# Attention with a gelu MLP on one core: the first group's maxima moved ahead of its exponentials, four groups' repeated parts written by copies inside DRAM

## Chip, cores and metric

The kernel runs on one core of one Trainium2 chip. The metric is the device time of one execution in microseconds (us); the time before is a median of three runs. An engine executes its instructions in the order in which they were written; the engines wait for each other by semaphores. TensorE is PE in the profile, its weight load PEld, VectorE DVE, ScalarE ACT, GpSimd POOL, and SyncE, which issues all DMAs here, SP.

## The reference, cut to what matters

`x` has 2048 rows of 512. `a` is attention with 32 heads of width 16, where each query sees itself and the 255 keys before it; `b` is a gelu MLP with 1792 hidden columns.

```
qkv = x @ wqkv                         # 2048 x 1536
p   = softmax(where(0 <= i - j < 256, q k^T / 4, -1e9))
a   = (p v) @ wo
b   = gelu(x @ w1 + b1) @ w2 + b2
g   = sigmoid((x * gate_w).sum(-1))
out = g * a + (1 - g) * b
```

## The kernel before, in words

All products are in a split form: a value is kept as a high part and the rest, and `mm3` (lines 108 to 110) multiplies high by high, high by rest and rest by high into the same sums. Lines 108 to 110 are therefore most of the PE work: q and k (tiles `qk`), v (`v`), the first MLP layer (`u`), the second (`y`) and the output projection (`a`).

**Stages.** The rows are four tiles of 512 (`t` = 0 to 3). `qkv(t)` transposes x (`xp`, line 261), makes q, k and v and stores them in DRAM. `qk_out` turns one 128-column piece `j` of q or k into two parts on ACT and DVE (tile `qke`, lines 322 and 325) and stores three: both parts (line 329), and the high part once more (line 330), so that the three products of the split form can later be stacked along the contraction axis. In SQ and SK the index `i` (0 to 3) is the piece: groups of four heads 0 to 3 read `i` 0 and 1, groups 4 to 7 read `i` 2 and 3. The space of `ks`, `qd` and `qs` serves as x transposed for `t` = 0, 1 and 2, and is cleared and loaded for attention afterwards.

**Attention** goes through eight groups of four heads, each in 16 blocks (`kb`) of 128 keys or queries, four instructions (`i`) per block. First the row maxima: `att_max` multiplies `qd` and `kd` (tile `sm`, line 519) and DVE takes the maximum under the mask (tile `jm`, line 524, with a small read-out row). `att_rows` negates and transposes four blocks' maxima (lines 536 to 539), and eight small casts on POOL put them as rows into `qs` (line 546). Then `att_exp` multiplies `qs` and `ks`, so that the maximum is taken off inside the product (tile `st`, line 564), ACT takes the exponential (tile `pt`, line 586), POOL cuts the band's corners (line 580), and `att_pvs` multiplies by v (line 608). `st`, `sm` and `d` (which holds `qk`, `u` and `y`) have 3, 3 and 2 buffers in PSUM.

**Order.** It is written out by hand with a counted clock. `fill(ns)` takes the next pieces of the dense work (qkv, then the MLP as `mlp`, then `final`) for that many ns; `after(ns, fn)` puts a step into a list that is worked off when the counted clock reaches it. The dense work runs alone for `START` = 105000 ns; `qd` is loaded `AHEAD` = 9000 ns before its end. The loop runs over `u` from -`LEAD` = -12: at each step it issues the maxima of block `u` + 12 and, from `u` = 0, the exponentials of block `u`; a quarter of `STEP0` (`u` below 0) or `STEP` is filled with dense work after each. In the MLP's first layer (`stage` "u") instructions go one by one, otherwise in pairs. So maxima stay 12 blocks ahead of exponentials all along, also at the start.

**The MLP's gelu** for one `u` tile has four ACT steps (x1 line 719, square 722, tanh 728, high part 734) and three DVE steps (725, 731, 737); x1 has two buffers. **Weights**: a raw weight tile is loaded (line 170), copied on ACT (178), and its rest taken on DVE or POOL (182, `split`). POOL takes odd tiles as long as the counted clock at the load is below `RAWS` = 152000; after it all go to DVE, with two raw buffers.

**DMAs** are all issued by SP in one order, with eight semaphores in turn: a DMA waits until the one eight before it has landed. `load_kd`, `load_qd`, `load_ks`, `load_qs` and `att_load_v` are written at fixed places of the loop; the first `load_ks` pair stands in `qkv(2)`, behind its pieces 8 and 9.

Of the kernel before, what the change touches and what calls it, by code (L numbers as in the profile page):

```python
# [19 lines left out]
NT = S // T  # L20
NB = T // 128
# [11 lines left out]
def gated_mix(ctx: ExitStack, tc: tile.TileContext, x, wqkv, wo, w1, b1, w2, b2, gate_w, out):  # L33
    nc = tc.nc
# [11 lines left out]
    def f32(ap):  # L46
        return ap.bitcast(F32)
# [187 lines left out]
    def clear_q(i):  # L235

        v = qd[:, i // 2, i % 2]
        nc.scalar.activation(v, nil.broadcast_to([128, 2 * T]), AF.Copy)

    xts, xrs = {}, {}  # L240

    def load_xr(t, bs=range(NB)):
# [71 lines left out]
    def qk_out(t, j, p):  # L314

        dst, i = (SQ[t], j) if j < NC else (SK[t], j - NC)
        e = sb.tile([128, 2, T], F32R, tag="h", bufs=7, name=f"qke{t}_{j}")

        h = 1 if j < NC else 0

        def hi():
            nc.scalar.activation(e[:, h], p, AF.Copy)  # L322

        def lo():
            nc.vector.tensor_sub(e[:, 1 - h], p, f32(e[:, h]))  # L325

        def store():
            to = dst[:, :, :, i].rearrange("h d s c -> (h d) s c")
            nc.sync.dma_start(to[:, 0:2], f32(e))
            nc.sync.dma_start(to[:, 2], f32(e[:, h]))  # L330
            done.add(("qk", t, j))
        after(100, hi), after(700, lo), after(700 + HOLDQ, store)

# [36 lines left out]
    def qkv(t):  # L370
# [30 lines left out]
        for n, (kind, j) in enumerate(pieces):  # L401
            if not last and XAT <= n < XAT + NC:
                nc.sync.dma_start(XT[t][n - XAT], f32(xts[t][:, n - XAT]))
            if kind == "qk":
                need(("w", (kind, j)))
            else:
                need(*[("w", ("v", c)) for c in range(NC)])
            if t == 0 and n == 10:
                nc.sync.dma_start(b1c, b1.rearrange("(f p) -> p f", p=128))
            if t == 0 and n < 2:  # L410
                pass
            elif kind == "qk":
                yield from qkv_qk(t, j)
            else:
                yield from qkv_v(t, j)
            if t == 1 and n % 3 == 2:
                clear_k(n // 3)
            if t == 2 and n < 4:
                clear_q(n)
            if t == 2 and n in (1, 2):  # L420
                load_kd(0, n - 1)
            if t == 2 and n in (8, 9):
                load_ks(0, n - 8)
            if t == 0:
                for i in ([2], [3], [4], [5], [6], [7, 8], [9, 10], [11])[n] if n < 8 else []:
                    split(keys[i], nc.vector if i % 2 else nc.gpsimd)
                if n == 1:
# [12 lines left out]
            if not last and n == xat[-1] + 1:  # L440
                gate(t + 1)
# [481 lines left out]
    for c in (0, 1):  # L923
        load_qd(0, c)
    fill(AHEAD)
    for u in range(-LEAD, NU):
        m = u + LEAD
        gm, bm = divmod(m, NKB)
        step = STEP if u >= 0 else STEP0
        for i in range(4):  # L930
            if i == 1 and m % NB == 0 and NB <= m < NU - NB:
                load_kd(*divmod(m // NB + 1, NT)), load_qd(*divmod(m // NB + 1, NT))
# [6 lines left out]
            for op, i in [(op, k) for k in pair for op in ORDER[:3]] + [("f", k) for k in pair]:  # L939
                if op == "s" and u >= 0:  # L940
                    att_exp(u // NKB, u % NKB, i)
                if op == "m" and m < NU:
                    att_max(gm, bm, i ^ XOR)
                if op == "p" and i == PVAT and u >= 1:
                    att_pvs(u - 1)
                if op == "f":
                    fill(step / 4)
        if m < NU and bm % RB == RB - 1:
            after(900, att_rows, gm, bm // RB)
        if m % NB == QAT % NB and QAT <= m < QAT + NKB:  # L950
            load_qs(0, (m - QAT) // NB)
# [18 lines left out]
WARM = (9, 4)  # L970
RB = 4
NKB = S // 128
PTS = 7
RAWS = 152000.0
PUT = 1200
LEAD = 12
QAT = 5
START = 105000.0
NORM = 6000
YSWAP = 3  # L980
GELU = (700, 1500, 3600, 4600, 6000, 7000)
XAT = 3
ORDER = 'mspf'
XOR = 1
PACE = 4000.0
LAND = 7500.0
# [6 lines left out]
DIVS = ((8000, 10000, 16000, 23000, 25000), (4500, 5700, 8500, 17000, 18500))  # L993
REST = 1000.0
MXAT = 5500.0
AHEAD = 9e3
STEP0 = 2750.0
PVAT = 2
STEP = 2330.0
# [20 lines left out]
```

## Time and profile before

| | us |
|---|---|
| median of three runs (lowest, highest) | 750.44 (749.94, 751.40) |
| the profiled execution's own time | 750.61 |
| its span | 748.9 |
| PE busy | 734.0 (98%) |
| DVE busy | 520.6 (70%) |
| ACT busy | 421.7 (56%) |
| POOL busy | 372.4 (50%) |
| DMA: moved, share of 16 engines | 170.97 MB, 81.3% |

The span runs from the first to the last instruction; 1.7 us of the execution lie around it. In a timeline a row has the start, the duration, the engine, the line, the operation, output<-input with shapes, a count, and in brackets how long the engine was idle before it and what ended that. Matmul rows overlap (a 512-column one is shown with 0.39 us, the next starts 0.23 us later), so prices of PE are taken from start to start.

### The profile page before, as it was taken

The page shows a single profiled execution, that of the slowest core. Times are in us where ns is not written, and L with a number is a line of the kernel's source. Part 1 is how long each engine was busy: PE and PEld are TensorE (multiplying, and loading weights), DVE is VectorE, ACT ScalarE, POOL GpSimd, SP SyncE. Part 2 cuts the span into 40 slices and gives each one's busy share as a digit, 9 for nine tenths or more (in the row PEclk, how much of TensorE's full clock was granted, in tenths as well). Part 3 has the DMA queues.
Part 4 walks back from the last instruction along what each step waited for, and adds up shares of the span by engine and source line. Part 5 has one row for each costly group of instructions (what it writes and reads, how often), then busy time and mean ns, then how long its engine had stood idle before and what let it go on. Part 6 is the DMA issues. An engine that isn't in the chain of part 4 may idle for free.

```text
span 748.9 us, 17963 instructions
## 1 busy us (share of the span) xinstructions
PE 734.0 (98%) x6129; PEld 606.7 (81%) x6129; DVE 520.6 (70%) x1567; ACT 421.7 (56%) x972; POOL 372.4 (50%) x846
## 2 busy tenths in 40 slices
PE   9999999998999999999999999999999999999998
PEld 7888888876788888888887887888888888878787
DVE  4532325799768867986798689768867886784552
ACT  4434532358537845764695478447735853784541
POOL 4200000339756865876587567747765875630000
PEclk9999999999999999999999999999999999999999
DMA  9889798997995777799676989996799799438682
GB/s 316 329 268 407 257 392 277 273 312 182 273 251 133 172 229 211 176 227 249 164 174 152 241 215 230 259 235 155 171 268 244 180 238 239 136 88 262 217 287 106
DMA packets 179259, 172.12 MB, mean 230 GB/s; under 512 B 56672, under 2 KB 122976, under 8 KB 179168
## 3 DMA queue, kind: packets, MB, share of 16 engines
q1 hardware_dynamic: 179168, 170.97, 81.3%
q8 instruction: 49, 0.80, 0.5%
q14 instruction: 42, 0.34, 0.2%
HBM read 108.53 MB, written 62.39 MB: 228 GB/s over the span
## 4 chain that ended last, share of the span: by engine, by line
PE 84%; DMA 4%; DVE 4%; ACT 3%; issue 3%; SPq 1%; POOL 1%; DVEq 0%; ACTq 0%; POOLq 0%
PE sm L519 9%; PE st L564 8%; PE pv_sm L608 7%; PE y L108 6%; PE y L109 6%; PE y L110 6%; PE u L108 6%; PE u L109 5%; PE u L110 5%; PE qk L110 4%; PE qk L108 4%; PE qk L109 4%; PE pv_st L608 2%; PE a L108 2%; PE v L108 2%
## 5 line engine op out<-in xcount | busy, mean ns | idle before, releaser
L524 DVE CUSTOM_DVE_ANT_0 jm<-sm,mask 128x320 bf16<-128x320 f32 (+4 forms) x512 | 238.0, 465 | 95.6 <-PE sm L519 61.2
L580 POOL TENSOR_SCALAR_AFFINE_SELECT pt<-pt 64x256 f32<-64x256 f32 (+1 forms) x538 | 228.1, 444 | 108.6 <-ACT pt L586 98.1
L586 ACT ACTIVATE pt<-st 128x320 f32<-128x320 f32 (+4 forms) x512 | 199.6, 424 | 138.7 <-PE st L564 136.1
L519 PE MATMUL sm<-kd,qd 96*128 96x320 f32 (+4 forms) x512 | 154.1, 312 | 6.0 <-DVE M L524 5.1
L564 PE MATMUL st<-qs,ks 128*128 128x320 f32 (+4 forms) x512 | 154.4, 309 | 1.7 <-ACT pt L586 1.7
L546 POOL CAST qs<-tt 4x256 fp32r<-4x256 f32 x256 | 124.2, 485 | 52.7 <-DVE tt L539 42.0
L519 PEld LDWEIGHTS sm<-kd,qd 96*128 96x128 f32 x512 | 96.5, 188 | 32.8 <-DVE M L524 13.5
L564 PEld LDWEIGHTS st<-qs,ks 128*128 128x128 f32 x512 | 97.5, 190 | 18.5 <-ACT pt L586 2.9
L108 PE MATMUL y<-w,h 128*128 128x512 f32 x224 | 88.6, 395 | 0.0
L109 PE MATMUL y<-w,h 128*128 128x512 f32 x224 | 88.1, 393 | 0.0
L110 PE MATMUL y<-w,h 128*128 128x512 f32 x224 | 87.9, 393 | 0.0
L108 PE MATMUL u<-mx,w 128*128 128x512 f32 x196 | 80.0, 408 | 0.0
L109 PE MATMUL u<-mx,w 128*128 128x512 f32 x196 | 77.4, 395 | 0.0
L110 PE MATMUL u<-mx,w 128*128 128x512 f32 x196 | 77.1, 393 | 0.0
L608 PE MATMUL pv_st<-pt,vbuf 64*32 64x320 f32 (+4 forms) x1408 | 73.3, 346 | 1.5 <-ACT pt L586 1.0
L608 PE MATMUL pv_sm<-pt,vbuf 64*32 64x320 f32 (+4 forms) x1408 | 74.2, 347 | 0.2
L608 PEld LDWEIGHTS pv_sm<-pt,vbuf 64*32 64x32 f32 x1408 | 51.2, 106 | 19.3 <-issue 2.2
L325 DVE TENSOR_TENSOR qke<-qk,qke 128x512 fp32r<-128x512 f32 x32 | 22.0, 689 | 46.9 <-ACT qke L322 31.1
L322 ACT ACTIVATE qke<-qk 128x512 fp32r<-128x512 f32 x32 | 19.1, 598 | 56.2 <-PE qk L110 30.3
L110 PEld LDWEIGHTS y<-w,h 128*128 128x128 f32 x224 | 42.1, 188 | 9.8
L608 PEld LDWEIGHTS pv_st<-pt,vbuf 64*32 64x32 f32 x1408 | 46.2, 106 | 1.8 <-ACT pt L586 1.1
L338 POOL MEMSET vx<- 128x32 f32 x16 | 2.4, 155 | 88.9 <-DMA SK<-qke 30.7
(148 smaller groups left out, 1334.7 us busy)
## 6 DMA issues: line engine op xcount, KB each, us to landing
kd<-SK SPq DMA_DIRECT2D x32, 384.0 KB
qs<-SQ SPq DMA_DIRECT2D x64, 192.0 KB
mx<-XT SPq DMA_DIRECT2D x24, 512.0 KB
SQ<-qke SPq DMA_DIRECT2D x16, 512.0 KB
SK<-qke SPq DMA_DIRECT2D x16, 512.0 KB
ND<-nd SPq DMA_DIRECT2D x32, 256.0 KB
raw_w<-in_B_w_dram SPq DMA_DIRECT2D x28, 256.0 KB
ks<-SK SPq DMA_DIRECT2D x32, 192.0 KB
```

The lines of the kernel that those rows point to most:

```text
L108: nc.tensor.matmul(p, lh, rh, start=first, stop=False)
L109: nc.tensor.matmul(p, lh, rl, start=False, stop=False)
L110: nc.tensor.matmul(p, ll, rh, start=False, stop=last)
L322: nc.scalar.activation(e[:, h], p, AF.Copy)
L325: nc.vector.tensor_sub(e[:, 1 - h], p, f32(e[:, h]))
L519: nc.tensor.matmul(p[:, :w], qd[0:96, n, pr, 128 * j:128 * (j + 1)], kd[0:96, n, pr, k1 - w:k1], start=True, stop=True)
L524: nc.vector.tensor_tensor_reduce(junk[:, :w], p[:, :w], mask[:, 320 - w:320], 1.0, -3e38, ALU.add, ALU.max, M[:, 2 * (b % RB) + hb, pr:pr ...
L546: nc.gpsimd.tensor_copy(dst, src.unsqueeze(1).broadcast_to([4, 2, RB, 32]))
L564: nc.tensor.matmul(p[:, :w], ks[:, slot(g_, kb // NB), pr, at:at + 128], qs[:, pr, k0:k0 + w], start=True, stop=True)
L580: nc.gpsimd.affine_select(out=v, in_=v, pattern=[[0, v.shape[1]], [1 - 2 * e, 64]], compare_op=ALU.is_ge, fill=0.0, base=-e, channel_multi ...
L586: nc.scalar.activation(pt[:, hf, pr, :w], p[:, :w], AF.Exp, scale=SCALE)
L608: nc.tensor.matmul(pv[r // 64][32 * i:32 * i + 32, q - c * T:e - c * T], vts[g_, b // NB][r:r + 64, v:v + 32], rhs(r), start=start, stop=s ...
```

## The change

Three things change, and the numbers that set their places:

- **Maxima.** The loop now starts at `u` = -16. A counter `made` and `next_max` issue maxima one by one. Before `u` = 0 all 64 maxima of the first group are issued (`4 * NKB`); from `u` = 0 a maximum is issued only when fewer than `4 * (u + 12)` + its place have been made. So none stands in blocks `u` = 0 to 3, and from `u` = 4 the maxima are 12 blocks ahead again. `START` goes from 105000 to 94000, `AHEAD` to 10000. `att_rows` comes 1400 ns after a quarter's last maximum instead of 900 ns after the whole step; the first group's `load_qs` come after blocks 5, 9, 13 and 15 instead of 5, 9, 13 and 17.
- **k's first stacks.** The first two `load_ks` move from `qkv(2)` to `qkv(3)`, behind its pieces 5 and 6 (the v tiles 1 and 2).
- **Copies.** For `i` = 2 and 3 (what groups 4 to 7 read) the repeated high part is no longer stored from SBUF. Sixteen DMAs copy it inside DRAM, from the part already stored, at counted times 188000, 196000 and so on to 308000.

```
-            nc.sync.dma_start(to[:, 2], f32(e[:, h]))
+            if i < 2:
+                nc.sync.dma_start(to[:, 2], f32(e[:, h]))
+                done.add(("qk", t, j))
+            else:
+                copies[0] += 1
+                after(COPY0 + COPY * copies[0] - now[0], copy, to)
+
+        def copy(to):
+            nc.sync.dma_start(to[:, 2], to[:, h])
             done.add(("qk", t, j))
...
-            if t == 2 and n in (8, 9):
-                load_ks(0, n - 8)
+            if last and n in (5, 6):
+                load_ks(0, n - 5)
...
-    for u in range(-LEAD, NU):
-        m = u + LEAD
+    made = [0]
+    def next_max():
+        m, i = divmod(made[0], 4)
+        made[0] += 1
         gm, bm = divmod(m, NKB)
+        if i == 1 and m % NB == 0 and NB <= m < NU - NB:
+            load_kd(*divmod(m // NB + 1, NT)), load_qd(*divmod(m // NB + 1, NT))
+        att_max(gm, bm, i ^ XOR)
+        if i == 3 and bm % RB == RB - 1:
+            after(1400, att_rows, gm, bm // RB)
+        if i == 3 and m in QAT:
+            after(600, load_qs, 0, QAT.index(m))
+    for u in range(-NKB, NU):
...
+            for k in pair:
+                if made[0] < (4 * (u + LEAD) + k + 1 if u >= 0 else 4 * NKB) and made[0] < 4 * NU:
+                    next_max()
+                if u >= 0:
+                    att_exp(u // NKB, u % NKB, k)
+                if k == PVAT and 1 <= u:
+                    att_pvs(u - 1)
+            for k in pair:
+                fill(step / 4)
...
+COPY0 = 180000.0
+COPY = 8000.0
-QAT = 5
-START = 105000.0
+QAT = (5, 9, 13, 15)
+START = 94000.0
-AHEAD = 9e3
+AHEAD = 10e3
```

**PE, at the first exponentials.** Before, from the first `st` on, each `st` (block, place) has an `sm` beside it; the `u` rows are the MLP's first layer:

```order
L519 MATMUL sm_12_1_1770<-kd,qd 128x320
L564 MATMUL st_0_0_1774<-qs,ks 128x320
L108 MATMUL u_2_1740<-xt_1009,w_2_1418 128x512
L109 MATMUL u_2_1740<-xt_1009,w_2_1418 128x512
L110 MATMUL u_2_1740<-xt_1009,w_2_1418 128x512
L519 MATMUL sm_12_0_1789<-kd,qd 128x320
L564 MATMUL st_0_1_1794<-qs,ks 128x320
L519 MATMUL sm_12_3_1797<-kd,qd 128x320
L564 MATMUL st_0_2_1802<-qs,ks 128x320
```

The same place in the changed kernel:

```order
L528 MATMUL sm_15_2_1827<-kd,qd 128x320
L108 MATMUL u_2_1806<-xt_1001,w_2_1476 128x512
L109 MATMUL u_2_1806<-xt_1001,w_2_1476 128x512
L110 MATMUL u_2_1806<-xt_1001,w_2_1476 128x512
L573 MATMUL st_0_0_1838<-qs,ks 128x320
L108 MATMUL u_2_1806<-xt_1001,w_2_1476 128x512
L109 MATMUL u_2_1806<-xt_1001,w_2_1476 128x512
L110 MATMUL u_2_1806<-xt_1001,w_2_1476 128x512
L573 MATMUL st_0_1_1848<-qs,ks 128x320
L573 MATMUL st_0_2_1850<-qs,ks 128x320
```

The 16 `sm` of blocks 12 to 15 have moved ahead of `st_0_0`; up to the `sm` just ahead of `st_4_0`, the next group's first, there is none. From `st_4_0` on PE's order is the same in both kernels.

**POOL, at the same place** (casts of row maxima into `qs`, a weight's rest, band corners of `pt`). Before:

```order
L182 TENSOR_TENSOR w_1_1749<-raw_w_1633,w_1_1749 128x512
L546 CAST qs<-tt 4x2x4x32 x2
L580 AFFINE_SELECT pt_0_1773<-pt_0_1773 64x4x64 x4
L546 CAST qs<-tt 4x2x4x32 x6
L182 TENSOR_TENSOR w_3_1884<-raw_w_1734,w_3_1884 128x512
L580 AFFINE_SELECT pt_1_1842<-pt_1_1842 64x4x64 x4
```

In the changed kernel:

```order
L182 TENSOR_TENSOR w_1_1815<-raw_w_1702,w_1_1815 128x512
L555 CAST qs<-tt 4x2x4x32 x2
L589 AFFINE_SELECT pt_0_1837<-pt_0_1837 64x4x64 x4
L555 CAST qs<-tt 4x2x4x32 x5
L589 AFFINE_SELECT pt_1_1883<-pt_1_1883 64x4x64 x4
L555 CAST qs<-tt 4x2x4x32
```

The rest of weight tile `w_3` is off POOL: its load now comes after the counted 152000, and DVE takes it. The casts here are those of the first group's last quarter; before, they were the third quarter's, and the last quarter's stood behind the corners of `pt_3`.

**SP, at the first load for the maxima** (XT is a store of x transposed, SQ and SK stores of q and k, `qd` and `ks` loads, SV stores of v). Before:

```order
L403 DMA XT_93<-qs 128x1024
L329 DMA SK_85<-qke_6_1035 128x2x512
L330 DMA SK_85<-qke_6_1035 128x512
L329 DMA SQ_81<-qke_3_1054 128x2x512
L330 DMA SQ_81<-qke_3_1054 128x512
L329 DMA SK_85<-qke_7_1079 128x2x512
L330 DMA SK_85<-qke_7_1079 128x512
L480 DMA ks<-SK_83 48x8x128
L475 DMA ks<-SK_83 48x7x128
L477 DMA ks<-SK_83 48x2x64
L357 DMA SV_89<-vx_0_1080 128x272
```

In the changed kernel:

```order
L412 DMA XT_93<-qs 128x1024
L489 DMA qd<-SQ_79 48x8x128
L484 DMA qd<-SQ_79 48x7x128
L486 DMA qd<-SQ_79 48x2x64
L489 DMA qd<-SQ_80 48x8x128
L484 DMA qd<-SQ_80 48x7x128
L486 DMA qd<-SQ_80 48x2x64
L330 DMA SK_85<-qke_6_1026 128x2x512
L330 DMA SQ_81<-qke_3_1050 128x2x512
L330 DMA SK_85<-qke_7_1074 128x2x512
L366 DMA SV_89<-vx_0_1075 128x272
```

The `qd` loads, which came 18 DMAs behind that store of XT, now follow it directly; the repeated parts and `ks` are gone from this place.

More of the change, by code (lines that the diff above doesn't have):

```diff
@@ L238, in clear_q @@
         nc.scalar.activation(v, nil.broadcast_to([128, 2 * T]), AF.Copy)
+    copies = [0]
     xts, xrs = {}, {}
@@ L925, in gated_mix @@
     fill(AHEAD)
-    for u in range(-LEAD, NU):
-        m = u + LEAD
+    made = [0]
+    def next_max():
+        m, i = divmod(made[0], 4)
+        made[0] += 1
         gm, bm = divmod(m, NKB)
+        if i == 1 and m % NB == 0 and NB <= m < NU - NB:
[6 more added lines that the diff above has]
+    for u in range(-NKB, NU):
         step = STEP if u >= 0 else STEP0
         for i in range(4):
-            if i == 1 and m % NB == 0 and NB <= m < NU - NB:
-                load_kd(*divmod(m // NB + 1, NT)), load_qd(*divmod(m // NB + 1, NT))
             if i % 2 == 0:
@@ L938, in gated_mix @@
                 pair = (i,)
[L939 to L944, printed above, removed]
-                    att_pvs(u - 1)
[L946 to L951, printed above, removed]
+            for k in pair:
[4 more added lines that the diff above has]
+                if k == PVAT and 1 <= u:
+                    att_pvs(u - 1)
+            for k in pair:
+                fill(step / 4)
         if u % NB == 0 and NB <= u < NU - NB:
@@ L982 @@
 XAT = 3
-ORDER = 'mspf'
 XOR = 1
```

## The prediction

> **What bounds the kernel now.** I read the page first: the span, the shares of the engines and the slices over time.
>
> ```profile
> span 748.9 us, 17963 instructions
> PE 734.0 (98%) x6129; PEld 606.7 (81%) x6129; DVE 520.6 (70%) x1567; ACT 421.7 (56%) x972; POOL 372.4 (50%) x846
> ...
> PE   9999999998999999999999999999999999999998
> ...
> DVE  4532325799768867986798689768867886784552
> ACT  4434532358537845764695478447735853784541
> ```
>
> PE sets the time. It is idle for 748.9 - 734.0 = 14.9 us of the whole span, so an edit that adds no PE work and takes none away can win that much at most, and only where the idle time lies in a place that it touches. One slice is 18.7 us. The first one that is not 9 is the tenth (168 to 187 us), and there DVE stands at 9 and ACT at 8. The profiled execution took 750.61 us, 1.7 more than its span and 0.17 more than the median of 750.44. I work from 750.61 and take the 0.17 off at the end.
>
> Next I asked for the busy time in four stretches: the maxima before the first exponential, the first `st` of block 0 to the last of block 4, the rest of that stage, and the time in which the copies will run. The columns are the length, then busy us of PE, PEld, DVE, ACT and POOL with counts, the granted clock, the DMA share and GB/s.
>
> ```profile
> 160.75:184.50 23.75, 20.91 (x161) 15.49 (x159) 22.18 (x63) 19.27 (x42) 18.25 (x32) 1.00 0.83 198
> 184.50:200.00 15.50, 14.53 (x112) 12.37 (x118) 13.15 (x43) 9.78 (x23) 11.97 (x27) 1.00 0.89 282
> 124.00:160.00 36.00, 36.00 (x173) 30.44 (x172) 28.12 (x102) 13.40 (x35) 10.93 (x21) 1.00 0.99 308
> 200.00:345.00 145.00, 144.93 (x1426) 121.60 (x1405) 111.57 (x370) 87.49 (x204) 99.23 (x232) 1.00 0.81 202
> ```
>
> From 124 to 160 us PE has no gap at all, although the DMA share is 0.99: the full DMA queues of the qkv stage cost PE nothing. From 160.75 to 184.50 PE is idle for 2.84 us and DVE is 93% busy; ACT has 4.48 us free (23.75 - 19.27). Here the change can win. The timeline of PE says who ends the waits:
>
> ```profile
> 160.60 0.31 PE L519 MATMUL sm<-kd,qd 96*128 96x320 f32 x1
> 160.75 0.32 PE L564 MATMUL st<-qs,ks 128*128 128x320 f32 x1
> 160.90 0.40 PE L108 MATMUL u<-xt,w 128*128 128x512 f32 x1
> ...
> 161.61 0.31 PE L519 MATMUL sm<-kd,qd 96*128 96x320 f32 x1
> ...
> 162.71 0.42 PE L519 MATMUL sm<-kd,qd 96*128 96x320 f32 x1 [0.65 <-DVE M L524]
> ...
> 167.42 0.41 PE L564 MATMUL st<-qs,ks 128*128 128x320 f32 x1 [0.30 <-ACT pt L586]
> ...
> 171.80 0.38 PE L564 MATMUL st<-qs,ks 128*128 128x320 f32 x1 [0.40 <-ACT pt L586]
> ...
> 176.53 0.42 PE L519 MATMUL sm<-kd,qd 96*128 96x320 f32 x1 [0.64 <-DVE M L524]
> ...
> 178.81 0.30 PE L519 MATMUL sm<-kd,qd 96*128 96x64 f32 x1 [0.44 <-DVE M L524]
> ...
> 181.73 0.24 PE L608 MATMUL pv_st<-nil,vbuf 64*32 64x64 f32 x1
> ```
>
> Four of the waits are `sm` for a PSUM buffer that DVE has not read yet or `st` for one that ACT has not read: both engines are near their limit, DVE more so.
>
> **The change, part by part.**
>
> **1. Maxima moved ahead of `st_0_0`.** By the order of PE, 15 `sm` of 320 columns that stood behind the first `st` now stand ahead of it (64 against 49). One costs 160.75 - 160.60 = 0.15 us, so `st_0_0` comes 15 x 0.15 = 2.25 us later, and this has to be earned back. On DVE a maximum of this width costs 0.49 + 0.08 us with its read-out:
>
> ```profile
> 158.16 0.49 DVE L524 CUSTOM_DVE_ANT_0 jm<-sm,mask 128x320 bf16<-128x320 f32 x1
> 158.58 0.08 DVE L524 DVE_READ_ACCUMULATOR2_ANT M<- 128x1 f32 x1
> ```
>
> In the stretch DVE falls from 22.18 to 22.18 - 15 x 0.57 = 13.6 us. Ahead of it DVE has 36.00 - 28.12 = 7.9 us free from 124 to 160, and more before that, against 8.6 to be placed and an earlier start; I cost this at nothing. If that cover failed, PE would wait there for what does not fit, 0.7 us.
>
> **2. What is late next: ACT.** Its work in the stretch does not change (the same 19 exponentials, gelu steps and four weight copies stand there in both orders), but PE passes through it with less of its own. PE's work from `st_0_0` to `st_4_3` is now 16 fills of three matmuls at 161.61 - 160.90 = 0.71, 19 `st` at 0.15, four narrow `sm` (0.2 by the pace of the wide ones) and the products with v, 1.9 us from 181.73 to the next `u` matmul:
>
> ```profile
> 183.63 0.50 PE L108 MATMUL u<-xt,w 128*128 128x512 f32 x1
> ```
>
> That is 11.4 + 2.85 + 0.2 + 1.9 = 16.4 us, less than ACT's 19.27. So the stretch cannot be run at PE's pace for long, and its length D is ACT's work, plus what ACT still stands idle, less the lead that PE may take on it (three `st` buffers). ACT's idle time before:
>
> ```profile
> 165.26 0.69 ACT L719 ACTIVATE x1h<-u,b1c 128x512 f32<-128x512 f32 x1 [1.50 <-DVE h L737]
> ...
> 175.29 0.69 ACT L719 ACTIVATE x1h<-u,b1c 128x512 f32<-128x512 f32 x1 [0.77 <-DVE h L737]
> ...
> 177.36 0.63 ACT L734 ACTIVATE h<-x1h 128x512 fp32r<-128x512 f32 x1 [0.48 <-DVE x1h L731]
> ```
>
> These three, 2.75 of the 4.48 us, stand behind DVE. To see whether DVE is late there because of the maxima, I looked at what it and POOL did just before:
>
> ```profile
> 160.10 1.60 POOL L182 TENSOR_TENSOR w<-raw_w,w 128x512 fp32r<-128x512 f32 x1 [6.79 <-ACT w L178]
> ...
> 173.41 1.29 POOL L182 TENSOR_TENSOR w<-raw_w,w 128x512 fp32r<-128x512 f32 x1
> ```
>
> ```profile
> 160.58 1.67 DVE L725 SCALAR_TENSOR_TENSOR sqh<-sqh,x1h 128x512 f32<-128x512 f32 x1
> ...
> 167.17 0.68 DVE L725 SCALAR_TENSOR_TENSOR sqh<-sqh,x1h 128x512 f32<-128x512 f32 x1
> ...
> 173.80 1.45 DVE L737 TENSOR_TENSOR h<-x1h,h 128x512 fp32r<-128x512 f32 x1
> ```
>
> A gelu step of 0.68 us took 1.67 and another 1.45 just when POOL took the rest of a weight tile. By the order, the second of these weight steps (`w_3`) goes to DVE and the first (`w_1`) stays on POOL at the same place. So the 0.77 and 0.48 behind the second should go; of the 1.50 I let 1.3 stand, since ACT will ask for x1's buffer sooner than before while DVE is as late; of the other 1.73 I let 0.7 stand. ACT's idle time is then 2.0. For the lead I take 1.2 us, three exponentials of 0.4 by their group's mean (424 ns):
>
> ```profile
> L586 ACT ACTIVATE pt<-st 128x320 f32<-128x320 f32 (+4 forms) x512 | 199.6, 424 | 138.7 <-PE st L564 136.1
> ```
>
> So D = 19.27 + 2.0 - 1.2 = 20.1, and the stretch wins 23.75 - 2.25 - 20.1 = 1.4 us. The ends: all of PE's waits gone, 23.75 - 2.25 - 16.4 = +5.1; ACT as idle as before and no lead, D = 23.75, that is -2.25.
>
> [...]
>
> **3. From 184.5 to 200 us** PE is idle for 0.97, the largest wait again an `sm` for DVE. The last quarter's negation, transposition and casts leave this place, but ACT arrives with a backlog. I take half, 0.5 us, between 0 and 1.0.
>
> **4. The first `qd` loads** come eleven counted us earlier, and the first `sm` stands behind the row at 108.18, at 108.4 us. In the order they follow directly on the fourth store of XT:
>
> ```profile
> 97.51 1.21 SPq L330 DMA_DIRECT2D SQ<-qke  x1
> 98.76 0.86 SPq L403 DMA_DIRECT2D XT<-qs  x1
> 99.72 0.86 SPq L329 DMA_DIRECT2D SK<-qke  x1
> 100.62 1.22 SPq L330 DMA_DIRECT2D SK<-qke  x1
> ```
>
> ```profile
> 108.18 0.39 PE L110 MATMUL v<-v,qs 128*128 128x512 f32 x1
> ```
>
> Three issues behind XT end at about 102 even without the 1.21 us of the removed store. The chain of waits shows what a load took in such a full queue:
>
> ```profile
> 159.80 5.81 DMA qs<-SQ
> ```
>
> That lands at 107.7, 0.7 us ahead of the need. I take nothing; the upper end is 2 us if it lands two later. The `ks` loads have some 30 us between piece 5 of `qkv(3)` and `st_0_0`; they move past weight loads on SP, which in turn gain from the missing stores. Nothing.
>
> **5. The copies.** Sixteen stores of 256 KB leave the qkv stage: 16 x 0.85 us at the 308 GB/s of 124 to 160, 13.6 us of a queue that cost PE nothing, so no gain. They come back from the first YA store on, by the order, and end behind the loads of the first `num` tiles:
>
> ```profile
> 201.16 0.42 SPq L816 DMA_DIRECT2D YA<-yo  x1
> ...
> 325.92 0.61 SPq L658 DMA_DIRECT2D num<-ND  x1
> ```
>
> From 200 to 345 the DMA share is 0.81 and PE idle for 0.07 of 145 us; 13.6 more raise it to 0.90, below the 0.99 at which PE had no gap. No trace shows a copy inside DRAM. At the low end it costs nothing; at the high end the two that fall into the fullest part push a load, 2 x 0.85 = 1.7 us. I take nothing: the nearest row is the stretch itself. Groups 4 to 7 read the copied part long after 326 us.
>
> **Sum.** 1.4 + 0.5 = 1.9 us: 750.61 - 1.9 = 748.7 for the profiled execution, 748.5 against the median.
>
> **The rivals.**
>
> *All waits go.* ACT fits its work into PE's pauses and PE's 5.1 and 0.97 us are won: 744.4. For it: DVE is the fuller engine now. Against it: ACT's 19.27 exceeds 16.4.
>
> *ACT takes DVE's place.* ACT keeps 3.3 of its 4.48 us idle, D = 21.4, and the second stretch wins nothing: 0.1 us, 750.3. For it: gelu goes to and fro between ACT and DVE, and PE's waits at 167.42 and 171.80 were for ACT already.
>
> *Slower: the 2.25 us are not paid back.* If ACT's pace decides and its idle time stays whole because each `x1` waits for DVE's `h` of two tiles before, the stretch keeps 23.75 us (22.55 with the lead) and begins 2.25 later: 751.5 to 752.7, about 752.1. It decides from D = 21.5 on. For it: the 1.50 us wait; against it: the relief of DVE.
>
> *The change doesn't hide its copies.* The 1.7 us of part 5 would take the forecast to 750.2.
>
> **How the numbers follow.** Chances: the forecast 0.42, all waits gone 0.10, ACT in DVE's place 0.25, slower 0.19, copies 0.04. A measurement can tell 0.2%, 1.5 us. Faster 0.42 + 0.10 = 0.52; same 0.25 + 0.04 = 0.29; slower 0.19. The range runs from 745.8 to 752.2: it leaves out the first rival and about half of the slower one, 0.19. The forecast's own range is 746.8 to 749.3 (D from 18.9 to 21).
>
> **What would show it.** Part 1: `st_0_0` 2.25 us later and no wait of PE from 108 to 163. Part 2: in the five blocks DVE near 14 us, waits of `st` for ACT in place of those of `sm` for DVE, ACT's row at the first x1 still waiting for `h`; a stretch of 20.1 us. Part 5: PE without gaps from 200 to 345 and a DMA share near 0.90. It is wrong if PE waits at the first `sm`, if the five blocks take over 21.5 us, or if new gaps appear behind 200 us.

## The result: 5.5 us slower

The changed kernel takes 756.38 us (median of six runs, 754.43 to 757.39), the kernel before 750.86 in the same runs: a ratio of 1.0068 with a 95% interval of 1.0051 to 1.0084. I had forecast 748.5 us and a range up to 752.2.

The page of the changed kernel's profiled execution, which took 757.39 us, shows the same PE work with more time around it (19.4 us idle instead of 14.9):

```profile
span 755.7 us, 17948 instructions
...
PE 736.3 (97%) x6129; PEld 608.6 (81%) x6129; DVE 523.3 (69%) x1568; ACT 422.0 (56%) x972; POOL 368.7 (49%) x845
...
PE   8999999988999999999999999999999999999998
```

The ninth and tenth slices stand at 8 (151 to 189 us); before, it was the tenth alone. The busy time by stretches, in the same columns as in the prediction: the five blocks, the time behind the first exponential, the seven us from 151 to 158, and the time of the copies.

```profile
168.75:190.42 21.67, 17.77 (x144) 13.51 (x143) 14.80 (x28) 18.73 (x42) 16.17 (x29) 1.00 0.48 112
...
151.01:158.00 6.99, 4.65 (x15) 3.60 (x14) 4.84 (x17) 1.71 (x3) 3.65 (x8) 0.76 0.83 264
200.00:345.00 145.00, 144.34 (x1443) 120.63 (x1442) 113.10 (x372) 87.69 (x203) 98.86 (x233) 1.00 0.90 233
```

The first row: DVE is down to 14.80 us and the blocks are 2.1 us shorter than before, not 3.65. The second is new: PE loses 2.3 us there and runs at a granted clock of 0.76. The third is what I forecast for the copies, but for a gap at 339 us.

PE's instructions are the same in both kernels, so the same matmul (the n-th of a kind) can be compared by its start. This is worked out from PE's timelines: how much later it starts than in the kernel before, in us. Each column is one execution: 757.39 us for the changed kernel, 755.08 for ks_early, 751.51 for rows_late, 749.65 for gelu_tight and 747.42 for casts_later. The first is the highest of its runs and the last two are the lowest of theirs, so the columns lie further apart than the medians.

| start before, us | changed | ks_early | rows_late | gelu_tight | casts_later |
|---|---|---|---|---|---|
| 103.17, `v` | 0.71 | 0.02 | -0.09 | -0.16 | 0.32 |
| 151.84, `u` | 8.15 | 3.30 | 2.48 | 2.40 | 2.87 |
| 163.96, `st` | 6.61 | 1.76 | 0.94 | 0.86 | 1.33 |
| 190.21, `st` | 5.66 | 0.80 | 0.66 | -0.43 | -2.43 |
| 301.66, `u` | 5.65 | 0.76 | 0.64 | -0.45 | -2.44 |
| 352.32, `st` | 6.44 | 1.45 | 0.66 | -0.47 | -2.46 |
| 523.90, `u` | 6.74 | 2.67 | 1.23 | -0.55 | -2.58 |
| 636.79, `u` | 7.33 | 3.23 | 1.22 | -0.60 | -2.66 |

(The other columns are experiments.) Of the changed kernel's 8.15 us at the first `u` tiles, 0.7 were there from the first 20 us on in this execution and belong to no edit, and 2.25 are the maxima ahead. The other 5.2 are a loss that no term of mine has. (In what follows, "the blocks" are the five from `st_0_0` to `st_4_3`.) After the blocks it grows again, at 335 us by 0.7 and near 474, 541 and 607 us by 0.3 each, far from the stretches that the prediction works out.

**The first loss, followed back.** SP's timeline between the fifth and the sixth load of a weight tile, in the kernel before:

```profile
132.45 0.59 SPq L170 DMA_DIRECT2D raw_w<-in_B_w_dram  x1
...
135.39 0.99 SPq L488 DMA_DIRECT2D kd<-SK  x2
136.42 0.45 SPq L480 DMA_DIRECT2D qd<-SQ  x1
...
137.94 0.43 SPq L170 DMA_DIRECT2D raw_w<-in_B_w_dram  x1
```

and in the changed kernel:

```profile
136.44 0.41 SPq L170 DMA_DIRECT2D raw_w<-in_B_w_dram  x1
137.24 0.33 SPq L489 DMA_DIRECT2D ks<-SK  x1
...
140.00 1.01 SPq L497 DMA_DIRECT2D kd<-SK  x2
141.07 0.44 SPq L489 DMA_DIRECT2D qd<-SQ  x1
...
144.26 0.60 SPq L489 DMA_DIRECT2D ks<-SK  x1
...
148.24 0.43 SPq L170 DMA_DIRECT2D raw_w<-in_B_w_dram  x1
```

In both orders a `kd` and a `qd` stand between the two weight loads (the third tile's before, the fourth tile's now, since the maxima run earlier). What is new in this place is both pairs of `ks` loads, six DMAs. The sixth weight tile leaves SP 10.3 us later, while PE is some 4 us late at that point. Then three engines wait in their order; ACT, DVE and PE of the changed kernel:

```profile
151.36 0.63 ACT L178 ACTIVATE w<-raw_w 128x512 fp32r<-128x512 f32 x1 [5.27 <-DMA raw_w<-in_B_w_dram]
151.90 0.58 ACT L323 ACTIVATE qke<-qk 128x512 fp32r<-128x512 f32 x1
152.51 0.69 DVE L326 TENSOR_TENSOR qke<-qk,qke 128x512 fp32r<-128x512 f32 x1 [3.18 <-ACT qke L323]
151.01 0.31 PE L528 MATMUL sm<-kd,qd 96*128 96x320 f32 x1
153.66 0.41 PE L528 MATMUL sm<-kd,qd 96*128 96x320 f32 x1 [2.34 <-DVE M L533]
...
154.60 0.63 PE L110 MATMUL qk<-xt,qk 128*128 128x512 f32 x1
155.03 0.63 PE L108 MATMUL qk<-xt,qk 128*128 128x512 f32 x1
```

ACT stands for 5.27 us at the copy of a weight that nobody needs yet, `qke` waits behind it, DVE waits for `qke` with maxima behind it, and PE waits for a buffer that a maximum frees: 2.5 us. Behind the gap matmuls of 512 columns follow at 0.43 us instead of 0.23 up to 157.6: some eight of them, 1.6 us more. Together 4.1 us in this execution; another 0.5 is lost at 124 us, of which below. Two of the six executions, 754.55 and 756.64 us, had a mean granted clock of 1.000 and the other four 0.997, so the 1.6 us of slow matmuls are not part of every execution.

### The profile page after: what moved, and what is told of

Its sections match the earlier page's. It is cut to its first block, busy times and chain, and to the rows that moved or that the text cites. A ratio compares the mean times of both kernels' runs of the same rounds, so it can differ in the third digit from the quotient of the medians.

```text
span 755.7 us, 17948 instructions
## 1 busy us (share of the span) xinstructions
PE 736.3 (97%) x6129; PEld 608.6 (81%) x6129; DVE 523.3 (69%) x1568; ACT 422.0 (56%) x972; POOL 368.7 (49%) x845
## 4 chain that ended last, share of the span: by engine, by line
PE 77%; DVE 7%; DMA 6%; issue 4%; ACT 3%; POOL 2%; SPq 1%; DVEq 0%; ACTq 0%; POOLq 0%
PE sm L528 9%; PE st L573 8%; PE pv_sm L617 6%; PE y L108 6%; PE y L109 6%; PE y L110 6%; PE u L108 5%; PE u L109 5%; PE u L110 5%; DVE jm L533 3%; PE qk L110 3%; PE qk L108 3%; PE qk L109 3%; PE pv_st L617 2%; PE a L108 2%
## 5 line engine op out<-in xcount | busy, mean ns | idle before, releaser
L555 POOL CAST qs<-tt 4x256 fp32r<-4x256 f32 x256 | 121.1, 473 | 59.7 <-DVE tt L548 29.4
L740 DVE SCALAR_TENSOR_TENSOR x1h<-sqh,x1h 128x512 f32<-128x512 f32 x56 | 42.0, 750 | 5.0 <-ACT sqh L737 4.9
```

The lines of the kernel that those rows point to most:

```text
L555: nc.gpsimd.tensor_copy(dst, src.unsqueeze(1).broadcast_to([4, 2, RB, 32]))
L740: nc.vector.scalar_tensor_tensor(x1, sq, 1.0, x1, op0=ALU.add, op1=ALU.mult)
```

## The experiments

All ratios are to the kernel before, timed beside it, with the 95% interval in brackets. Three theories stood at the start: 1, the moved `ks` loads delay weight loads; 2, the 2.25 us are not paid back because ACT paces the blocks; 3, the copies.

**ks_early**: the changed kernel with `ks` loaded where it was.

```
-            if last and n in (5, 6):
-                load_ks(0, n - 5)
+            if t == 2 and n in (8, 9):
+                load_ks(0, n - 8)
```

> The changed kernel with k's first stacks loaded where they were before (in qkv(2), behind its pieces 8 and 9); maxima and copies as changed. Theory 1, the weight loads: behind the moved ks loads the sixth raw weight tile left SP at 148.24 us instead of 137.94, ACT waited 5.27 us for it, and PE stood 2.3 us at 153.66 and then ran at a clock of 0.91. With ks out of the way that tile leaves SP near 140, ACT waits less than 1 us for a weight, PE has no gap from 140 to 160, and the time is 756.4 - 4.1 = 752.3 us. Theory 2, the 2.25 us of maxima are not paid back by the stretch: ks matters little, 755.5 to 756.5. Theory 3, the copies: unchanged, 756.4.

753.99 us, 1.0031 (1.0019 to 1.0043), 1.7 us over theory 1's 752.3. The wait is gone: ACT's waits for weights from 120 to 170 us are now

```profile
ACT w L178 <- DMA raw_w<-in_B_w_dram: 0.4, 1, 0.4
```

and the table's 8.15 falls to 3.30. So by the ratios 0.37% of the 0.68% was this, 2.8 us (the two kernels were not timed beside each other); the rest stands.

**no_copies**: `if i < 2:` becomes `if True:`, all parts stored from SBUF.

> The changed kernel with all repeated parts stored from SBUF again, no copy inside DRAM; maxima and ks as changed. Theory 1: sixteen stores return to the queue of the qkv stage, four of them while qkv(3) runs, so the weight loads come no earlier; the wait at 151 stays, the time is 756 to 758 us. Theory 3, the copies are the loss: the new gap at 339 us (0.49) and those behind 380 go, and the time falls to 752 to 753.

755.69 us, 1.0057 (1.0036 to 1.0078), not clear of the changed kernel's 1.0068. The copies are not the loss; the steps behind 335 us are there without them. Theory 3 falls. Theory 1 expected the wait at 151 us to stay: it stays, but takes 1.08 us instead of 2.34, so its size hangs on the whole queue and not on `ks` alone.

**maxima_alone**: both of these edits, so that of the change only the maxima's part is left.

> The first part of the change alone: maxima ahead, START, AHEAD and the first qs loads as changed; ks early and all parts stored from SBUF as before. Theory 1: no wait at 151 us, 752 us or a little less (2.25 us later at the first st, 2.1 won in the five blocks). Theory 2: 753 to 755, since its loss is the maxima's. Theory 3: 751, as nothing but the copies costs.

755.12 us, 1.0046 (1.0030 to 1.0063); theory 1's 752 missed. With the stores back ACT waits for weights 8.3 us in six places although `ks` is early. So `ks` alone does not decide when a weight arrives; the stores in the same queue do too.

**split_later**: all loads stay where the change has them; only ACT's copy of the first weight tiles, and the rest that is taken behind it, are written later.

```
-            after(LAND + 1500, split, key, ...
+            after(LAND + 5500, split, key, ...
```

> The changed kernel with the ACT copy of the first weight tiles placed 4 counted us later in ACT's order (13 instead of 9 us behind the load's place), all loads where the change has them. Theory 1 in its narrow form, that the loss is ACT standing in order at a weight copy while qke waits behind it: ACT's waits at 151.36 and 158.83 shrink from 5.27 and 2.97 us to 1 us or less, the PE gap at 151 goes though ks is as late as before, 752 to 753 us. If instead the full DMA queue delays something else that PE needs, the time stays at 756.

755.05 us, 1.0047 (1.0030 to 1.0063). The mechanism holds: no weight copy of ACT waits for its load any more, and there is no gap at 151, with loads as late as before; the first `u` starts 3.65 us late instead of 8.15. The time is 2 us and more over theory 1's, and its interval overlaps the changed kernel's: the blocks win back only 1.3 us instead of 2.5. That the weight copies now lie in the blocks is a likely reason; no run tests it.

**ks_late_alone**: the kernel before with `ks` late and nothing else.

> The kernel before with one edit: k's first stacks loaded behind pieces 5 and 6 of qkv(3). Theory 1 in its plain form, that six more DMAs in this part of SP's queue are enough: a weight tile leaves SP over 8 us later than the 137.94 of before, ACT waits for it, PE has a gap near 150 us, and the time is 752.5 to 755. If it takes the maxima's loads (kd and qd of the third and fourth tile, which the change moves into the same 20 us) as well: less than 1 us, 751 to 752.

753.73 us, 1.0030 (1.0017 to 1.0043). The move is enough by itself to lose time, but not as expected: the sixth weight tile leaves SP at 139.36 us, 1.4 us later than before and not over 8, and the next six 2.1 to 3.2 us later. ACT waits for weights 1.87, 1.13 and 1.78 us, the last one at 161 us, and PE's gap lies at the first exponentials and not near 150 us:

```profile
164.17 0.41 PE L519 MATMUL sm<-kd,qd 96*128 96x320 f32 x1 [2.10 <-DVE M L524]
...
164.86 0.63 PE L109 MATMUL u<-xt,w 128*128 128x512 f32 x1
```

**The second loss** has its place in a line of the change that I had read as a detail: the maxima's negation and transposition come 1400 counted ns behind a quarter's last maximum instead of 900 behind the whole step, for all eight groups. DVE at 332 us, the kernel before:

```profile
331.84 0.48 DVE L524 CUSTOM_DVE_ANT_0 jm<-sm,mask 128x320 bf16<-128x320 f32 x1
...
332.89 0.17 DVE L536 TENSOR_SCALAR nm<-M 128x16 fp32r<-128x16 f32 x1
333.10 0.18 DVE L537 SCALAR_TENSOR_TENSOR nm<-M,nm 128x16 fp32r<-128x16 f32 x1
333.38 0.45 DVE L539 STREAM_TRANSPOSE tt<-nm 128x256 f32<-128x256 f32 x1
333.75 0.45 DVE L524 CUSTOM_DVE_ANT_0 jm<-sm,mask 128x320 bf16<-128x320 f32 x1
```

and with the new place (ks_early; DVE, then PE):

```profile
331.52 0.49 DVE L533 CUSTOM_DVE_ANT_0 jm<-sm,mask 128x320 bf16<-128x320 f32 x1
...
332.55 0.26 DVE L545 TENSOR_SCALAR nm<-M 128x16 fp32r<-128x16 f32 x1
332.84 0.21 DVE L546 SCALAR_TENSOR_TENSOR nm<-M,nm 128x16 fp32r<-128x16 f32 x1
333.16 0.45 DVE L548 STREAM_TRANSPOSE tt<-nm 128x256 f32<-128x256 f32 x1
333.53 0.45 DVE L533 CUSTOM_DVE_ANT_0 jm<-sm,mask 128x320 bf16<-128x320 f32 x1
...
334.05 0.30 PE L617 MATMUL pv_sm<-pt,vbuf 64*32 64x64 f32 x2 [0.60 <-DVE M L533]
```

The three steps, about one us together, now stand two maxima further ahead, and the products with v wait for the buffer which the first of these two maxima frees.

**rows_late**: ks_early with these steps at their old place.

```
-        if i == 3 and bm % RB == RB - 1:
-            after(1400, att_rows, gm, bm // RB)
...
+        if made[0] // 16 > made0 // 16:
+            gm, bm = divmod(made[0] // 4 - 1, NKB)
+            after(900, att_rows, gm, bm // RB)
```

> The changed kernel with ks early, and with the maxima's negation and transposition (three DVE instructions, some 1.1 us together) placed again where the kernel before has them, 900 counted ns behind the whole step instead of 1400 behind the quarter's last maximum. Theory R: with ks early 2.6 us are still lost, because these three stand ahead of a maximum whose buffer the next sm or pv_sm needs. They show as steps of PE's delay at 124 (0.7), 335 (0.7), 443 (0.4 to 1.1), 474, 541 and 607 us (0.3 each), with waits of 0.33 to 0.91 for DVE M. Then these steps go, and the time is 753.99 - 2.5 = 751.5 us. Theory 2, only the ACT pace in the five blocks costs: 754, unchanged.

751.55 us, 1.0003 (0.9993 to 1.0014). The steps at 335, 474, 541 and 607 us are gone from the table, and so is the wait of 0.33 us at 124. With the edits of ks_early and rows_late the time is the kernel before's again, within the interval.

**rows_early_alone**: the kernel before, with the 1400 ns place.

> The kernel before with one edit: the negation and transposition come 1400 counted ns behind the quarter's last maximum instead of 900 behind the whole step. Theory R: new waits for DVE M ahead of pv_sm or sm, at 334 us among others, and 1.5 to 3 us more than before: 753 to 754. If the place of these steps matters only together with the rest of the change: 751.3, as before.

752.46 us, 1.0009 (0.9998 to 1.0020). In its trace PE falls back by 0.70, 0.33, 0.32 and 0.31 us at 335, 474, 541 and 607, as foreseen. The median is below the 753 to 754 expected, and the interval includes no change: by itself this place is seen in the trace (1.66 us together) and not in the times. The step at 124 us, which the changed kernel has, is not there: it needs the maxima ahead.

**copies_alone**: the kernel before with the copies.

> The kernel before with one edit: the sixteen repeated parts of groups 4 to 7 are copied inside DRAM. Copies hidden, as I forecast: 751.3, between 0.5 less (a lighter queue in the qkv stage) and nothing. Theory 3, copies push loads behind 200 us: 752 to 753, with PE gaps from 200 to 345 us that end on a DMA.

751.68 us, 1.0014 (1.0000 to 1.0027). From 200 to 345 us the delay stays between 0.39 and 0.55 us: the copies are hidden, as forecast. Near 443 us its trace is up to 3 us later and gives 1.2 back; ks_late_alone, ks_early and rows_late have such a step there too, the changed kernel has none. DVE's timeline names the cause, a load that DVE waits for in its order with maxima behind it:

```profile
442.89 0.69 DVE L671 TENSOR_TENSOR num<-num,rb 128x512 f32<-128x512 f32 x1 [2.11 <-DMA rb<-RD]
```

The same instruction waits 1.76 us in ks_late_alone, 1.40 in ks_early and 0.77 in rows_late, and not at all in the kernel before and the changed kernel. In copies_alone and ks_late_alone 3.4 us at half the clock follow. Why the load lands later in some executions stays open.

**maxima_rows_late**: rows_late with all parts stored from SBUF.

> The maxima's move by itself: ks early, negation placed as before, all repeated parts stored from SBUF as before. By the trace of the 751.55 us kernel the first st comes 2.5 us later and 1.85 are won back by the end of the five blocks: 751.3 + 0.65 = 751.9 us. If the copies pay for the maxima by a lighter queue in the qkv stage: 752.5 to 753, with weight waits of ACT as in the run of the maxima alone. My forecast of a gain of 1.9 us would be 749.4.

754.26 us, 1.0040 (1.0026 to 1.0053). The second expectation by its sign, 1.3 us beyond its range: ACT waits for weights 11.7 us in seven places, against one wait of 1.3 us in rows_late. In this pair the copies are worth 0.37% (1.0040 against 1.0003), because they take stores out of the fullest part of the queue. I had costed that relief at nothing. The size holds for this pair alone: maxima_alone against ks_early gives 0.15%, and no_copies against the changed kernel nothing that is clear of the intervals.

**The third question**: why do the five blocks win 2.1 us and not 3.65? **w1_dve** takes POOL's weight step away (`key != ("w2", 1)` in the choice of engine, on rows_late).

> The changed kernel with ks early and the negation and transposition placed as before (751.55 us), and the rest of weight tile w_1 taken on DVE instead of POOL. In my prediction the first idle time of ACT in the five blocks, 1.5 us at x1, stands because DVE's gelu step beside POOL's weight step takes 1.46 to 1.67 us instead of 0.68. If so that step falls to 0.7, ACT's wait falls to about 0.7 (DVE takes the 0.7 us weight step itself), the five blocks take 20.7 to 21.4 instead of 21.7 us, and the time is 750.6 to 751.3. If the wait has another cause, nothing changes: 751.5.

751.59 us, 1.0001 (0.9988 to 1.0014). The gelu step beside it falls from 1.71 to 0.69 us and ACT's longest wait at x1 from 1.7 to 1.22, but from 164 to 190 us its trace wins only 0.3 us more than rows_late's. That trace has 3.4 us at half the clock from 174.46, which rows_late's has not and which hides part of the gain; the medians are equal all the same (751.59 and 751.55).

**more_dense** gives each of the first four blocks 3000 ns of dense work (`step = STEP0 if u < 0 else 3000.0 if u < 4 else STEP`), **both** has the two edits.

> As the kernel of 751.55 us, with 3000 instead of 2330 ns of dense work per block in the first four blocks of exponentials (u = 0 to 3), so that exponentials come more slowly to ACT there. Theory 2, ACT's pace bounds the five blocks now: PE's waits for ACT pt (1.36 and 2.16 us) shrink by 2 us or more, as 2.7 us more of PE's dense work lie in the blocks; the dense work is only moved, so the time falls by those 2 us, to 749.5, if the end of the program doesn't miss the work. If it is not ACT's pace but the order of its steps, the waits stay and the time is 751.5 or, with less dense work beside the last group, up to 1 more.

> The two edits together on the kernel of 751.55 us: the rest of w_1 on DVE and 3000 ns of dense work per block in the first four. If both do what their theories say, 748.8 us, and PE's waits in the five blocks fall below 1.5 us in all; if the two gains are the same idle time, 749.5; if neither holds, 751.5.

752.89 us, 1.0016 (1.0006 to 1.0026), and 752.63 us, 1.0013 (1.0003 to 1.0023). PE's waits for ACT in the blocks do not shrink (1.52, 1.16, 0.78 and 1.02 us in more_dense, against 1.36, 2.16 and 0.48 in rows_late): dense work here is gelu work for ACT too. But in its trace the time is lost at the end of the program: PE waits 1.53 us at 697.81, runs at half the clock for 3.4 us behind that, and waits 0.81 us more at 726.71. At the first output projections, between the two, it is still 0.9 us ahead of rows_late; at the end it is 0.5 us behind. The dense work that was moved into the blocks is likely what is missing there. So the remedy did not help the whole, and what it is worth in the blocks by itself stays open.

**w_on_dve** copies six weight tiles' high parts on DVE instead of ACT (`nc.vector.tensor_copy(w[:, 0], raw)` for the second layer's tiles 1 to 6), **w_on_dve_w1** has the edit of w1_dve too.

> The kernel of 751.55 us (ks early, negation placed as before), with the high parts of weight tiles w_1 to w_6 of the second layer copied on DVE instead of ACT: about five copies of 0.52 us leave ACT in and just ahead of the five blocks, and DVE, 14.9 of 21.7 us busy there, takes them. If ACT's amount of work bounds the blocks: ACT falls from 18.2 to 16 us, PE's waits for ACT pt (1.36 and 2.16 us) shrink by about 2 us, 749.5 to 750. If ACT waits for DVE's gelu steps rather than being full: DVE gets later, the waits stay, 751.5 to 752.5.

> The same with the rest of w_1 on DVE too, so that no weight step on POOL stretches the gelu step (1.71 us against 0.69). Both theories on ACT: another 0.3 us less than w_on_dve, as in the run with that edit alone; 749.2 to 749.7. If DVE is now the fuller engine: up to 0.5 more than w_on_dve.

754.44 us, 1.0039 (1.0024 to 1.0055), and 753.43 us, 1.0024 (1.0009 to 1.0039). The first is slower than both of its expectations, and the second is 1.0 us below the first, where 0.3 below or up to 0.5 above was expected. The five blocks of rows_late (up to 0.6 us ahead of `st_4_3`), and those of w_on_dve (up to 1.2 us ahead of it):

```profile
163.08:184.79 21.71, 17.17 (x141) 13.05 (x140) 14.86 (x28) 18.25 (x41) 16.40 (x29) 1.00 0.46 108
```

```profile
163.48:185.90 22.42, 17.00 (x130) 12.69 (x128) 18.12 (x34) 16.20 (x36) 16.89 (x29) 1.00 0.46 113
```

ACT has 2 us less to do and PE no less to wait. That speaks against the amount of ACT's work as the bound in this order, though it does not settle it, since DVE has 3.3 us more to do. The order of ACT's steps was left. ACT in the kernel before, and in the changed kernel (tanh is L728 before and L737 in the changed kernel, x1 L719 and L728, the square L722 and L731):

```profile
168.40 0.66 ACT L728 ACTIVATE sqh<-sqh 128x512 f32<-128x512 f32 x1
168.92 0.46 ACT L586 ACTIVATE pt<-st 128x320 f32<-128x320 f32 x1
169.54 0.69 ACT L719 ACTIVATE x1h<-u,b1c 128x512 f32<-128x512 f32 x1 [0.16 <-DVE h L737]
```

```profile
176.87 0.69 ACT L728 ACTIVATE x1h<-u,b1c 128x512 f32<-128x512 f32 x1 [0.54 <-DVE h L746]
177.45 0.62 ACT L178 ACTIVATE w<-raw_w 128x512 fp32r<-128x512 f32 x1
177.97 0.62 ACT L737 ACTIVATE sqh<-sqh 128x512 f32<-128x512 f32 x1
178.49 0.68 ACT L731 ACTIVATE sqh<-u,b1c 128x512 f32<-128x512 f32 x1
179.06 1.44 ACT L595 ACTIVATE pt<-st 128x320 f32<-128x320 f32 x4
```

Before, tanh stands ahead of the next tile's x1 with an exponential between them. Now it stands behind an x1 that waits for DVE, and four exponentials wait behind tanh and square; PE's largest wait (2.16 us, at 179.64) ends with the first of them. The reason that I found is the counted clock: a `u` tile counts 12 x 227 = 2724 ns, and the 4.7 `st` that fall on it 146 each, some 3.4 us in all; with an `sm` beside each `st` it was 4.1. But gelu's steps keep their counted distances.

**gelu_tight** multiplies these distances by 0.83 (3.4 / 4.1) for the tiles that are made once 56 of the first group's 64 maxima are issued, up to the end of block 3 (`after(ns * tight, fn)`), on rows_late; **gelu_tight_w1** has the edit of w1_dve too.

> The kernel of 751.55 us (ks early, negation placed as before) with the distances between the gelu steps multiplied by 0.83 for the tiles of the first layer that are made while no maxima are issued; each tanh then stands ahead of the next tile's x1 on ACT again, as in the kernel before. Theory G, the order: ACT's row of x1, tanh and square in one piece ahead of the exponentials goes, PE's waits for ACT pt (1.36 and 2.16 us) fall to under 1.5 in all, the blocks take 19.5 to 20.1 us, near my forecast, and the time is 749.5 to 750. If the chain between ACT and DVE itself binds (x1 has two buffers): the waits stay near 3.5 us, 751.5.

> The same, with the rest of weight tile w_1 on DVE, so that the first gelu step isn't stretched (1.71 against 0.69 us). Theory G: with the order mended the 1.0 us counts more than the 0.3 us it did alone, since ACT's first x1 waits for this chain: 748.8 to 749.5. If the chain binds: 751.3.

750.63 us, 0.9994 (0.9982 to 1.0005), and 751.69 us, 1.0003 (0.9992 to 1.0014). In gelu_tight PE's waits for ACT fall to 1.34 us, as expected. From `st_0_0` to `st_4_3` it takes 21.34 us instead of rows_late's 22.34, not the 20.1 expected, because the next engine steps in. The gain is read from the traces: the interval overlaps rows_late's. gelu_tight_w1, expected at 748.8 to 749.5, is no faster at all; PE has the same wait for POOL (1.31 us), and in its trace 3.4 us at half the clock follow from 184.92. PE in gelu_tight:

```profile
171.52 0.38 PE L573 MATMUL st<-qs,ks 128*128 128x320 f32 x1 [0.98 <-ACT pt L595]
176.62 0.42 PE L573 MATMUL st<-qs,ks 128*128 128x320 f32 x1 [0.36 <-ACT pt L595]
181.94 0.40 PE L617 MATMUL pv_sm<-pt,vbuf 64*32 64x128 f32 x2 [1.30 <-POOL pt L589]
```

**casts_later**: gelu_tight, with the first group's last quarter negated, transposed and cast 10 counted us later, so that POOL's eight casts stand behind the corners of block 3.

```
-            after(900, att_rows, gm, bm // RB)
+            after(11000 if made[0] == 64 else 900, att_rows, gm, bm // RB)
```

> The kernel with ks early, negation placed as before and gelu steps at 0.83 (750.63 us), with the first group's last quarter negated, transposed and cast 11000 instead of 900 counted ns behind its maxima, so that its eight casts on POOL (0.6 to 0.7 us each) come behind the corners of pt_3 and not between those of pt_0 to pt_2. If these casts hold up the corners: the waits of 1.30, 0.20 and 0.18 us for POOL pt go or fall under 0.5 in all, the first st of block 4's last place comes 1.2 to 1.7 us earlier, 749.2 us. If POOL is late because ACT's exponentials are: the waits stay, 750.6.

749.19 us, **0.9971 (0.9956 to 0.9985)**: the expected number, and a kernel that is faster than the one before, clear of the interval. Its page, its `st_0_0` and `st_4_3`, and its five blocks:

```profile
span 745.7 us, 17945 instructions
...
PE 732.3 (98%) x6129; PEld 605.9 (81%) x6129; DVE 520.6 (70%) x1568; ACT 421.8 (57%) x972; POOL 370.9 (50%) x845
```

```profile
163.47 0.30 PE L573 MATMUL st<-qs,ks 128*128 128x320 f32 x1
...
182.13 0.36 PE L573 MATMUL st<-qs,ks 128*128 128x320 f32 x1
```

```profile
163.47:182.13 18.66, 17.31 (x144) 13.54 (x143) 14.62 (x30) 18.01 (x42) 12.68 (x23) 1.00 0.52 128
```

No wait for POOL is left and the five blocks take 18.66 us, less than the 20.1 that I had forecast. The step is 2.7 us, more than the 1.2 to 1.7 expected of it. ACT is now busy for 18.01 of these 18.66 us: here its amount of work is nearly the whole length, as the prediction took it to be. The whole change wins 0.29%, some 2.2 us, once four places are put right: the `ks` loads, the negation, gelu's distances and the casts. What the maxima's move is worth without the copies stays open; on rows_late the copies were needed.

## Why the prediction was wrong, point by point

**Part 1, the maxima ahead.** The 2.25 us were right: with the other causes removed, rows_late is 2.48 us late at 151.84 us. "I cost this at nothing" was right for the maxima (no wait of PE from 108 to 163 in rows_late) and wrong for the steps behind them: I counted that the last quarter's negation leaves the blocks, not where the negations arrive. Their new place cost a 0.33 us wait at 124 and the steps from 335 us on, 0.28% between ks_early and rows_late (1.0031 and 1.0003, not timed beside each other).

**Part 2, the five blocks.** Forecast 20.1 us; measured 21.67, just beyond the 21.5 from which my slower rival decides. DVE's relief came (14.80 us for "near 14"), waits of `st` for ACT in place of those of `sm` for DVE too, and x1 waits 1.48 us where I let 1.3 stand. The terms that failed: ACT is idle for 21.67 - 18.73 = 2.94 us instead of 2.0, and PE's lead of 1.2 us was not there (the exponential of `st_4_3` starts 0.4 us behind it). ACT's 19.27 was too high, which hid part of this: the same 42 instructions occupy 18.73 us here and 18.01 in casts_later. The step that led to them is "Its work in the stretch does not change (the same 19 exponentials, gelu steps and four weight copies stand there in both orders)": the same set, but not the same order, and then POOL's casts. The traces of gelu_tight and casts_later show both; in the times only the two together are clear of the intervals. In the rows of the kernel before, five waits of PE are shown, not four. The gelu step beside POOL's weight step stayed stretched: 1.46 us beside a weight step of 1.39 in the changed kernel, and 0.69 without one in w1_dve. How the one slows the other no run shows. Its price was small, as w1_dve's median shows (751.59 us against rows_late's 751.55).

**Part 3.** Forecast 0.5 us; the delay goes from 5.92 at `st_4_3` (190.42 - 184.50) to 5.66, that is 0.26.

**Part 4, the loads.** The `qd` loads cost nothing, as forecast: no wait at the first `sm`, at 109.11 us. (By `START` less `AHEAD` they come twelve counted us earlier, not eleven.) **The step that failed most is "they move past weight loads on SP, which in turn gain from the missing stores. Nothing."** I looked at whether `ks` would land in time for its own reader and not at what is queued behind the weights that it delays: ACT's copy in order, `qke` behind it, a maximum behind that. By the ratios it was 2.8 us between the changed kernel and ks_early, 2.3 us in ks_late_alone. A DMA share of 0.99 without a gap, which I took for a sign that the queue costs nothing, only said that it cost nothing in that order.

**Part 5, the copies.** Right where it looked: a DMA share of 0.90 from 200 to 345 us, and the one gap there, at 339, is also there without copies. Its other half, that taking the stores out of the qkv stage wins nothing because the queue cost PE nothing, failed beside the early maxima: 0.37% between maxima_rows_late and rows_late.

**Rivals.** "ACT takes DVE's place" comes nearest for the blocks (21.4 us against 21.67). No rival held the late weight or the place of the negation, the two that made the sign.

## What to carry to other kernels

When loads are moved on a queue that issues in order, price what they pass: follow the delayed DMA to its reader, then what stands behind that reader on its engine, up to the engine that sets the end. When a program's order comes from a counted clock, every instruction taken out of a stretch shortens the count there, and steps at fixed counted distances change places; compare the order of every engine at each place, not the sets of instructions. After each bound that is removed, ask for the next one by name: here DVE, then ACT's order, then POOL's casts, then ACT's amount of work.

## What the runs showed of the hardware

**A gap of PE can cost more than its length.** The 3.41 us that hold most of the changed kernel's 2.34 us wait, and the 3.41 us behind them (columns as above; the granted clock is the third number from the end):

```profile
150.68:154.09 3.41, 1.07 (x6) 0.69 (x5) 1.44 (x4) 1.11 (x2) 1.27 (x1) 1.00 0.81 250
154.09:157.50 3.41, 3.41 (x10) 2.75 (x10) 2.95 (x13) 0.60 (x1) 1.97 (x5) 0.50 0.84 277
```

At the clock of 0.50 matmuls followed at 0.43 us instead of 0.23. The traces of all kernels together have twelve such stretches between the first 12 us and the last 20, each 3.41 us long. In the 3.41 us ahead of each one PE was busy for 1.0 to 2.0 us. The length of the wait alone does not decide: a wait of 1.45 us in copies_alone (445.25, PE busy for 1.88 of 3.41 us) was followed by one, the wait of 2.16 us at 179.64 in the changed kernel (1.76 of 3.41 us) was not. The same `st` waits 2.16 us in w1_dve (1.25 busy, followed) and in rows_late (1.54 busy, not followed). Nor does PE's busy time ahead: followed at 1.25 and 1.88 us, not followed at 1.54 and 1.76. What sets such a stretch off is not shown.

**The releaser named by a trace can be a neighbour.** In w_on_dve PE's wait of 1.91 us at 174.22 is put down to POOL's cast; the same `st` waits as long for ACT's exponential in rows_late (2.16), and ACT's first one of four starts at 173.64 in w_on_dve. I take it for the same wait; the runs don't prove it.
